# Weight rounding rescheduled over two blocks: earlier tiles and three more of them in block 0, one VectorE step per slot in block 1

## The chip, the cores and the metric

The kernel runs on one core of a Trainium2 chip. The metric is device time in microseconds (us), the median of several runs. A core has TensorE (PE; its weight loads are listed as PEld), VectorE (DVE), ScalarE (ACT), GpSimd (POOL) and SyncE (SP), which here issues most transfers. Each has a queue of its own that it works through in order.

## The reference

An attention without softmax, a normalisation, and two matrix products with a leaky relu between them:

```python
kv = np.einsum('bhsd,bhse->bhde', k, v)          # 8 batches, 8 heads, 576 tokens, 64 wide
out = np.einsum('bhsd,bhde->bhse', q, kv)
rms = np.sqrt(np.mean(out * out, axis=-1, keepdims=True) + 1e-06)
x = (out / rms * g_norm)                          # rearranged to 4608 tokens x 512
h = x @ w_in                                      # 512 x 2048
g = np.maximum(0.01 * h, h)
return g @ w_out                                  # 2048 x 512
```

All is float32, but the two weight matrices arrive as float64. The kernel turns them into float32 itself, from the two 32-bit halves of each number; it calls that rounding.

## The kernel before

**Blocks and chunks.** The 4608 tokens are worked in nine blocks of 512 (`NT`). The 2048 hidden columns are four chunks (`NC`) of 2 x 256. A unit is one block and one chunk: its first product (h), the leaky relu, and its second product (o). Both products are done by a Strassen scheme with seven products in place of eight, so each needs sums and differences of its inputs, made on GpSimd and VectorE.

**Order of the work.** Block 0's chunks 0 to 2 come first, as plain products, in `first_block` (L1120): twelve steps n, each with a group of eight matmuls into `h_ps`, and a group of eight into four accumulators `o_acc` for the step before. Then the loop at L1232 takes block 1 with all four chunks, block 0 with its last chunk, and blocks 2 to 8. A unit of the loop has seven slots, one per Strassen product of h; the o products of earlier units are put between them, after a lag of two slots (`go_o`, L1224). The slot number is `at = 7 * now + t`; the seven products come in the order 1, 2, 6, 5, 7, 3, 4. Products 1, 6, 7 and 4 share one PSUM bank, and 2, 5 and 3 another. Product 5 begins its bank afresh, so it waits until product 2 has been read from it.

**Rounding.** There are 32 jobs (`w_jobs`), each for 128 x 512 weights: 0 to 23 for chunks 0 to 2, 24 to 27 for chunk 3's `w_out`, 28 to 31 for its `w_in`. A job (`round_f64`, L245) is loaded raw by SP (`load_w`), then takes six instructions: two on ScalarE (L263 `add`, L261 `cut`), VectorE L265, ScalarE L270, VectorE L280 and L283. `round_w` (L315) issues the first three and then finishes the job before; `finish_w` issues the rest. In block 0 a table `plan` says what is issued in each half step (n, 0) before and (n, 1) after the o group's place: a number is a job, "f" is `finish_w`, "t" and "a" are steps of two attention generators, "x" is the set of differences of block 1's tokens (`sides_x`). In block 1, `W_SLOTS` lists the slots at which a job is begun; in other slots `finish_w` is called. The group for step n of block 0 needs job 2n-1 for h, and o_acc of step m needs job 2m+2.

**Attention for batch 1** is a generator of steps: transposes of q (`turn`, L500), k-v products, `copy_kv` (L368), two `outputs` (L403), and `divide` (L423): two transposes with reductions, a root (L433), a reciprocal with two spreads, then twice a transpose and a product (L447, L449).

**GpSimd.** Its work for block 1 begins with L1191, a one-element copy that waits for the last of the differences of `sides_x`. Then come the Strassen sums of the weights (`sides_w1`, L699; `sides_w2`, L735), a second level of them (`combine`, L778), which is written to DRAM for the later blocks, and the sums of each unit's g (`sums_of`, L915). In block 1, GpSimd's instructions keep program order. `combine` puts its sums into places listed in `stage_homes`; its third part is done by VectorE at the slots of `DIRECT`.

**Order on the engines.** `pin` keeps an instruction in program order on its engine. The rest (many copies and additions to o) are put between by a planner at compile time, by its own cost estimates. The roundings and the additions to g (L937 to L945) are pinned.

**Homes of the raw weights.** `raws` are seven places of 4 KB per partition (three in `stage`, four in `pairs`), used in turn for jobs 0 to 23; later jobs use two halves of `early`, a token tile that is free by then, and places of `stage`.

Of the kernel before, what the change touches and what calls it, by code (L numbers as in the profile page):

```python
# [24 lines left out]
def kernel(  # L25
# [36 lines left out]
    nc = tc.nc  # L62
# [12 lines left out]
    NC = DF // 2 // (U * P)  # L75
# [37 lines left out]
    def view(t, lo, *shape):  # L113
        n = 1
        for d in shape:
            n *= d
        t = t[:, lo:lo + n]
        names = "abcd"[:len(shape)]
        return t.rearrange(f"p ({' '.join(names)}) -> p {' '.join(names)}",
                           **dict(zip(names, shape))) if len(shape) > 1 else t  # L120
# [97 lines left out]
    def spare(n, name, dtype=F32):  # L218
# [4 lines left out]
    raws = [view(stage, i * NW, NW) for i in range(3)] + [pair(i, NW) for i in range(4)]  # L223
    raw_homes = itertools.chain(
        itertools.islice(itertools.cycle(raws), 4 * K * U),
        itertools.cycle([early[:, :NW], early[:, NW:], raws[0], raws[1], raws[2]]))

    def load(t, src, eng):

# [71 lines left out]
    def load_w(j, *eng):  # L301
        eng = eng or (nc.sync,)
        dst, src = w_jobs[j]
        if w_in.dtype == I64:
            w_raws[j] = load_f64(src.bitcast(U32), eng)
        else:
            load(dst, src, eng)
# [115 lines left out]
    def divide(lo, hi, sums):  # L423

        x, n = x_of(lo, hi), hi - lo
        rms = work.tile([P, 2, n // E], F32, tag="rms", name="rms", bufs=2)
        for l in range(2):
            t = t2k(n, "turned")
            in_turn(nc.vector.transpose(t, sums[l]))
            in_turn(nc.vector.tensor_reduce(rms[:, l, :], t.rearrange("p (a i) -> p a i", i=E),  # L430
                                            axis=AX.X, op=ALU.add))
            if l:
                act = nc.scalar.activation(rms, rms, func=AF.Sqrt, scale=1.0 / D, bias=eps_sb)  # L433
                if first_done or in_first:
                    pin(act)
            yield
        in_turn(nc.vector.reciprocal(rms, rms))
        spread = []
        for l in range(2):
            t = t2k(n, "spread")  # L440
            first_turn(nc.scalar.copy(t.rearrange("p (a i) -> p a i", i=E),
                                      rms[:, l, :].unsqueeze(2).to_broadcast([P, n // E, E])))
            spread.append(t)
        yield
        for l in range(2):
            inv = t2k(n, "inv")
            in_turn(nc.vector.transpose(inv, spread[l]))  # L447
            to = x[:, 2 * l:2 * l + 2, :]
            in_turn(nc.vector.tensor_mul(to, to, inv.unsqueeze(1).to_broadcast([P, 2, n])))  # L449
            yield  # L450
# [243 lines left out]
    def add(eng, out_, a, b_, minus=False, pinned=False):  # L694
        ins = eng.tensor_tensor(out_, a, b_, op=ALU.subtract if minus else ALU.add)  # L695
        if pinned or steady or (in_block_1 and eng is nc.gpsimd):
            pin(ins)
# [37 lines left out]
    def sides_w2(n):  # L735
# [7 lines left out]
        def sums(i):  # L743
# [15 lines left out]
            else:  # L759
# [12 lines left out]
    NG = 7 * P  # L772
    SLOT = {1: 0, 2: 1, 4: 2, 5: 3, 6: 4, 7: 5, 3: 6}
    w1_dram = [dram.tile([P, 7, 7, P], F32, name=f"w1_{c}") for c in range(NC)]
    stage_homes = iter([view(w1_all, (6 + i) * NW, NW) for i in (0, 1, 0, 1)]
                       + [view(stage, i * NW, NW) for i in (1, 2, 0, 1, 2, 0, 1, 2, 0, 1, 2, 0)])

    def combine(c, part):  # L778


        direct = w1_sb[0][c].rearrange("p u (t r) m -> p u r t m", t=2)
        last = w1_sb[1][c][:, :, 2:, :].unsqueeze(3)
        parts = [((5, 6), pair(0, U, 2, 2, P))], [((7, 3), pair(1, U, 2, 2, P))], \
            [((1, 2), direct), ((4,), last)]

        eng = nc.vector if part == 2 else nc.gpsimd
        for js, y in parts[part]:
            t = view(next(stage_homes), 0, 4, len(js), P)
            s1, s2, s3, s4 = (t[:, i, :, :] for i in range(4))
            y11, y12, y21, y22 = (y[:, u, r, :, :] for u in range(2) for r in range(2))  # L790

            add(eng, s1, y21, y22, pinned=part == 2)
            add(eng, s2, s1, y11, True, pinned=part == 2)
            add(eng, s3, y11, y21, True, pinned=part == 2)
            add(eng, s4, y12, s2, True, pinned=part == 2)
            to = w1_dram[c][:, :, AT[js[0]]:AT[js[0]] + len(js), :]
            if js[0] == 1:
                for r in range(2):
                    put_off(to[:, r, :, :], y[:, 0, r, :, :])
            else:  # L800
                put_off(to[:, :2, :, :], y[:, 0, :, :, :])
            put_off(to[:, 2, :, :], y22)
            put_off(to[:, 3:, :, :], t)
# [316 lines left out]
    def first_block(between):  # L1120
# [27 lines left out]
        for t in range(4):  # L1148
# [8 lines left out]
    tail, a_steps = tail_of(0, NT, S, True), attention(1, False)  # L1157
    t, a, f, x = "tafx"
    plan = {(1, 0): (5, f, t), (1, 1): (t, 6, f, t), (2, 0): (t, 7, f, t), (2, 1): (8, f, t, t),
            (3, 0): (9, f, a), (3, 1): (10, f), (4, 0): (11, f, a), (4, 1): (12, f),  # L1160
            (5, 0): (13, f, a), (5, 1): (14, f), (6, 0): (15, f), (7, 0): (16, f, a, a),
            (7, 1): (17, f, a, a), (8, 0): (18, f, a), (8, 1): (19, a, f, a),
            (9, 0): (20, a, f), (9, 1): (21, a, f, a), (10, 0): (22, f), (10, 1): (23, f, x)}
    loaded, x_sides = 12, None

    def between(n, half):
        nonlocal loaded, x_sides
        for what in plan.get((n, half), ()):
            if what == f:
                finish_w()  # L1170
            elif what == x:
                x_sides, _, sums, _ = sides_x(1)
                go(sums)
            elif what in (t, a):
                go(tail if what == t else a_steps, 1)
            else:
                round_w(what)
                to = what + 7 if what < 19 else what + 5
                while loaded <= min(to, 28):
                    load_w(loaded)  # L1180
                    loaded += 1
                    if loaded in (13, 16):
                        load_pair(1, {13: 2, 16: 3}[loaded], homes=homes_1[{13: 2, 16: 3}[loaded]])
# [2 lines left out]
    first_block(between)  # L1186
    in_first = False
    first_done = True
    rounded = 24
    in_block_1 = True  # L1190
    pin(nc.gpsimd.tensor_copy(pair(0, NW)[:1, :1], x_sides[4][:1, 0, :1]))  # L1191
    h_sides, more = sides_w1(0)
# [4 lines left out]
        sides_w2(0)[1](part)  # L1197
    in_loop = True

    W_SLOTS = (1, 3, 5, 7, 10, 11, 13, 14)  # L1200
    LATE_ONE = {15: 2, 16: 1}
    A_SLOTS = {18: 1, 19: 1, 20: 1, 23: 1, 24: 1, 25: 1, 26: 1, 27: 1, 28: 1, 29: 1, 34: 2}
    DIRECT = {15: 0, 20: 1, 23: 2, 26: 3}
    READS = {20: 2, 24: 4, 28: RING}
    PARTS = {33: ("11", "12"), 35: ("22",), 37: ("21",)}

# [25 lines left out]
    for i, chunks in rounds:  # L1232
# [7 lines left out]
        for c in chunks:  # L1240
# [4 lines left out]
                product_h_two(i, c, now, quarters, g_sides, second_of(now - 2))  # L1245
            for t in range(7):
                slot = 7 * c + t
                go(h_steps, 1)
                if not one:

# [39 lines left out]
                    read(READS[at])  # L1290
                if one:
                    if at in DIRECT:
                        combine(DIRECT[at], 2)
                    if t == 3 and nxt[0] < 2 and nxt[1] != c:
                        h_sides, more_h = sides_w1(nxt[1])
                        combine(nxt[1], 0)
                    if t == 5 and nxt[0] < 2 and nxt[1] != c:
                        more_h()
                        combine(nxt[1], 1)
                    if at in W_SLOTS:  # L1300
                        round_w(rounded)
                        rounded += 1
                        if loaded < len(w_jobs):
                            load_w(loaded)
                            loaded += 1
                    else:
                        finish_w()
                    if at in (15, 16):
                        load_pair(2, at - 15)
                    go(late, LATE_ONE.get(at, 0))  # L1310
                    go(a_steps, A_SLOTS.get(at, 0))
                    load_some()
                    if at == 7 * NC - 4:
                        x_sides, _, sums, _ = sides_x(0)
                        go(sums)
                    elif at == 7 * N1 - 4:
                        x_sides, new_quarters, sums, inner = sides_x(2)
                        go(sums)
                    elif at == 7 * N1 - 3:
                        inner(0)  # L1320
                    elif at == 7 * N1 - 2:
                        inner(1)
# [44 lines left out]
```

## Time and profile before

| what | value |
|---|---|
| median of 3 runs | 932.97 us (932.75 to 933.2) |
| profiled execution: time, span | 932.04 us, 930.3 us |
| mean granted TensorE clock | 0.998 |
| PE, PEld busy | 909.7 us (98%), 784.5 us (84%) |
| VectorE, ScalarE, GpSimd busy | 628.6 us (68%), 347.3 us (37%), 375.7 us (40%) |
| TensorE works on block 0's steps | from 24.6 to 120.9 us |
| block 1's first h group begins | 120.88 us |

The span runs from the first to the last instruction of the profiled execution; its own time is a little longer. An engine's busy share is a mean over stages with different limits, so the stages are read one by one. A line such as "PE a L1 <- DVE b L2" says that a TensorE instruction writing `a` waited and that VectorE's instruction at L2, writing `b`, came last. In a list by time the columns are start, duration, engine, line, operation, output, input, shape, number, and in brackets the idle time before it. L126 is the helper that records every matmul and L695 the one that records every addition, so these are told apart by the tiles they write.

### The profile page before, as it was taken

What the parts mean: (1) busy time and instruction counts of PE and PEld (TensorE: products, weight loads), DVE (VectorE), ACT (ScalarE), POOL (GpSimd) and SP (SyncE); (2) the same over time, 40 slices, a digit from 0 to 9 for tenths busy, and PEclk for the clock granted to TensorE, in tenths of its full rate; (3) what the DMA queues carried; (4) which work ended last, traced back from release to release, by engine and by line L of the source; (5) the groups of instructions that cost most, each with busy time, mean ns of one, the idle gap of its engine ahead of it and who ended that gap; (6) DMA issues with size and microseconds to landing.
All of it is one profiled execution on the core that took longest, in us unless ns stands there. A gap on an engine that the chain in (4) does not pass through costs nothing.

```text
span 930.3 us, 18159 instructions
## 1 busy us (share of the span) xinstructions
PE 909.7 (98%) x7024; PEld 784.5 (84%) x7024; DVE 628.6 (68%) x1151; ACT 347.3 (37%) x679; POOL 375.7 (40%) x443
## 2 busy tenths in 40 slices
PE   8998889899999999999999999999999999999998
PEld 4543368688898999999999999999999999999997
DVE  5673745978575877577856786688658755765565
ACT  5764545313234422433334324333343333223330
POOL 2000199864623275226322632255225622552222
PEclk9999999999999999999999999999999999999999
DMA  9996264599689678877887778757765676567632
GB/s 253 243 266 183 68 216 165 180 336 311 206 277 312 212 227 251 249 236 223 252 259 230 215 222 263 234 176 219 238 187 172 188 225 199 185 187 219 200 116 91
DMA packets 92405, 202.16 MB, mean 217 GB/s; under 512 B 10016, under 2 KB 44448, under 8 KB 92320
## 3 DMA queue, kind: packets, MB, share of 16 engines
q1 hardware_dynamic: 81344, 189.14, 68.3%
q10 hardware_dynamic: 10528, 10.69, 3.4%
q8 instruction: 56, 0.92, 0.4%
q0 software_dynamic: 448, 1.18, 0.3%
q14 instruction: 29, 0.24, 0.1%
HBM read 173.44 MB, written 27.53 MB: 216 GB/s over the span
## 4 chain that ended last, share of the span: by engine, by line
PE 81%; DMA 8%; DVE 6%; ACT 2%; issue 1%; SPq 1%; POOL 0%; DVEq 0%; ACTq 0%; POOLq 0%
PE o_c L126 18%; PE o_a L126 18%; PE h_ha L126 11%; PE h_hb L126 10%; PE h_hc L126 8%; PE h_hd L126 8%; PE o_ps L126 3%; DMA v_in<-in_v_dram 2%; DMA q_in<-in_q_dram 1%; DMA pairs<-in_moe_w_in_dram 1%; DMA stage<-in_moe_w_in_dram 1%; PE h_a L126 1%; DMA pairs<-in_v_dram 1%; PE h_c L126 1%; DVE g L695 1%
## 5 line engine op out<-in xcount | busy, mean ns | idle before, releaser
L695 POOL TENSOR_TENSOR gs<-g 128x512 f32<-128x512 f32 x66 | 85.3, 1292 | 255.7 <-ACT g L908 255.7
L908 ACT ACTIVATE g<-g 128x512 f32<-128x512 f32 x127 | 80.1, 631 | 142.0 <-DVE g L695 142.0
L1027 ACT COPY w_all<-h_ha 128x512 f32<-128x512 f32 x84 | 49.0, 583 | 169.2 <-PE h_ha L126 163.6
L126 PE MATMUL o_c<-pairs,gs 128*128 128x256 f32 x392 | 93.3, 381 | 1.8 <-DVE o L695 1.8
L126 PE MATMUL o_a<-pairs,gs 128*128 128x256 f32 x392 | 93.0, 380 | 0.0
L695 DVE TENSOR_TENSOR o<-h_hb,o 128x128 f32<-128x128 f32 x104 | 29.9, 287 | 83.4 <-ACT pairs L1027 83.3
L126 PEld LDWEIGHTS o_c<-pairs,gs 128*128 128x128 f32 x392 | 71.2, 190 | 11.6 <-issue 2.2
L695 DVE TENSOR_TENSOR o<-o_a,o 128x512 f32<-128x512 f32 (+1 forms) x93 | 62.5, 672 | 23.7 <-PE o_a L126 23.3
L126 PEld LDWEIGHTS o_a<-pairs,gs 128*128 128x128 f32 x392 | 71.3, 190 | 8.1
L695 DVE TENSOR_TENSOR o<-o_c,o 128x512 f32<-128x512 f32 x80 | 54.7, 684 | 25.4 <-PE o_c L126 25.2
L126 PE MATMUL h_ha<-stage,w_all 128*128 128x128 f32 x448 | 59.6, 276 | 0.0
L126 PEld LDWEIGHTS h_ha<-stage,w_all 128*128 128x128 f32 x448 | 56.6, 192 | 3.0 <-issue 0.7
L695 DVE TENSOR_TENSOR g<-g,pairs 128x512 f32<-128x512 f32 x84 | 55.7, 689 | 1.9
L695 POOL TENSOR_TENSOR pairs<-g 128x128 f32<-128x128 f32 x52 | 23.8, 458 | 75.9 <-PE h_hb L126 47.4
L695 DVE TENSOR_TENSOR w_all<-h_hc,w_all 128x512 f32<-128x512 f32 x56 | 38.4, 685 | 15.9 <-PE h_hc L126 15.8
L695 DVE TENSOR_TENSOR o<-h_hd,o 128x128 f32<-128x128 f32 x78 | 22.2, 284 | 38.0 <-ACT pairs L1027 37.9
L126 PE MATMUL h_hb<-stage,w_all 128*128 128x128 f32 x336 | 46.7, 275 | 0.0
L126 PE MATMUL o_acc<-w,g 128*128 128x512 f32 x96 | 43.8, 599 | 2.9 <-DVE w L283 2.9
L695 POOL TENSOR_TENSOR gs<-g,gs 128x512 f32<-128x512 f32 x33 | 45.8, 1386 | 0.0
L695 POOL TENSOR_TENSOR gs<-gs,g 128x512 f32<-128x512 f32 x33 | 44.6, 1351 | 2.6
L1027 ACT COPY pairs<-h_hb 128x384 f32<-128x384 f32 x84 | 40.1, 477 | 13.6 <-PE h_hb L126 13.2
L126 PE MATMUL h_ps<-xT,w_all 128*128 128x512 f32 (+1 forms) x104 | 44.0, 569 | 0.1
(242 smaller groups left out, 2237.2 us busy)
## 6 DMA issues: line engine op xcount, KB each, us to landing
w_all<-w SPq DMA_DIRECT2D x196, 448.0 KB, 4.2
pairs<-w SPq DMA_DIRECT2D x56, 512.0 KB, 4.4
out_dram<-o ACTq DMA_DIRECT2D x35, 256.0 KB, 4.5
v_in<-in_v_dram SPq DMA_DIRECT2D x27, 288.0 KB, 4.9
k_in<-in_k_dram SPq DMA_DIRECT2D x26, 288.0 KB, 4.3
q_in<-in_q_dram SPq DMA_DIRECT2D x52, 144.0 KB, 5.7
q_in<-in_q_dram SPq DMA_DIRECT2D x52, 140.0 KB, 5.7
stage<-in_moe_w_out_dram SPq DMA_DIRECT2D x8, 512.0 KB, 6.7
```

The source lines that it names most:

```text
L126: pin(nc.tensor.matmul(*args, **kw))
L695: ins = eng.tensor_tensor(out_, a, b_, op=ALU.subtract if minus else ALU.add)
L908: nc.scalar.activation(t, t if src is None else src, func=AF.Prelu, alpha=SLOPE)
L1027: nc.scalar.copy(q[:, at], bank)
```

## The change

The table for block 0 is rewritten. Job 16 goes to the half step (6, 1), which was empty, and each later job one half step earlier; from (7, 0) on, the attention steps stand ahead of the job in their half step, not behind it. The root of `divide` becomes a step of its own while block 0 runs. Jobs 24, 25 and 26 are done in steps 11 and 12. The raw weights of jobs from 24 on use three homes in turn, where it was five; `combine`'s second and third places become two of `stage`, where they were in `w_all`. In block 1 the five jobs left are begun in slots 0, 3, 6, 9 and 12: L263, L261 and L265 in the first slot, L270 ahead of the h product of the second and L280 behind it, L283 in the third. VectorE's part of `combine` is split in two over two slots, the differences of `sides_x` likewise, and the rest of batch 1's attention moves from slots 15 and 16 to 17 and 19.

```diff
-        itertools.cycle([early[:, :NW], early[:, NW:], raws[0], raws[1], raws[2]]))
+        itertools.cycle([early[:, :NW], early[:, NW:], raws[0]]))
...
             if l:
+                if in_first:
+                    yield
                 act = nc.scalar.activation(rms, rms, func=AF.Sqrt, scale=1.0 / D, bias=eps_sb)
...
-    stage_homes = iter([view(w1_all, (6 + i) * NW, NW) for i in (0, 1, 0, 1)]
-                       + [view(stage, i * NW, NW) for i in (1, 2, 0, 1, 2, 0, 1, 2, 0, 1, 2, 0)])
+    stage_homes = iter([view(w1_all, (6 + i) * NW, NW) for i in (0, 1)]
+                       + [view(stage, i * NW, NW) for i in (1, 2, 1, 2, 0, 1, 2, 0, 1, 2, 0, 1, 2, 0)])
...
-            [((1, 2), direct), ((4,), last)]
-
-        eng = nc.vector if part == 2 else nc.gpsimd
+            [((1, 2), direct)], [((4,), last)]
+
+        eng = nc.vector if part > 1 else nc.gpsimd
...
-            (3, 0): (9, f, a), (3, 1): (10, f), (4, 0): (11, f, a), (4, 1): (12, f),
-            (5, 0): (13, f, a), (5, 1): (14, f), (6, 0): (15, f), (7, 0): (16, f, a, a),
-            (7, 1): (17, f, a, a), (8, 0): (18, f, a), (8, 1): (19, a, f, a),
-            (9, 0): (20, a, f), (9, 1): (21, a, f, a), (10, 0): (22, f), (10, 1): (23, f, x)}
+            (3, 0): (9, f, t, a), (3, 1): (10, f), (4, 0): (11, f, a), (4, 1): (12, f),
+            (5, 0): (13, f, a), (5, 1): (14, f), (6, 0): (15, f), (6, 1): (16, f),
+            (7, 0): (a, a, 17, f), (7, 1): (a, 18, f), (8, 0): (a, 19, f), (8, 1): (a, 20, f),
+            (9, 0): (a, a, 21, f), (9, 1): (22, a, f), (10, 0): (a, 23, a, f), (10, 1): (a, x),
+            (11, 0): (24, f), (11, 1): (25, f), (12, 1): (26, f)}
...
-                to = what + 7 if what < 19 else what + 5
-                while loaded <= min(to, 28):
+                to = what + 7 if what < 17 else max(24, what + 3)
+                while loaded <= min(to, 31):
...
-    rounded = 24
+    rounded, rest = 27, collections.deque()
...
-    W_SLOTS = (1, 3, 5, 7, 10, 11, 13, 14)
-    LATE_ONE = {15: 2, 16: 1}
+    LATE_ONE = {17: 2, 19: 1}
...
-    DIRECT = {15: 0, 20: 1, 23: 2, 26: 3}
+    DIRECT = {15: 0, 16: 1, 20: 2, 21: 3, 22: 4, 23: 5, 26: 6, 27: 7}
...
+                if rest:
+                    go(steps, rest[0][0])
                 go(h_steps, 1)
...
-                        combine(DIRECT[at], 2)
+                        combine(DIRECT[at] // 2, 2 + DIRECT[at] % 2)
...
-                    if at in W_SLOTS:
-                        round_w(rounded)
+                    if not rest and rounded < len(w_jobs):
+                        steps = rounding(rounded)
+                        rest.extend(((0, 3), (2, 1), (0, 1)))
                         rounded += 1
-                        if loaded < len(w_jobs):
-                            load_w(loaded)
-                            loaded += 1
-                    else:
-                        finish_w()
+                    if rest:
+                        go(steps, rest.popleft()[1])
+                    if loaded < min(rounded + 3, len(w_jobs)):
+                        load_w(loaded)
+                        loaded += 1
...
-                        go(sums)
                     elif at == 7 * N1 - 4:
                         x_sides, new_quarters, sums, inner = sides_x(2)
-                        go(sums)
-                    elif at == 7 * N1 - 3:
+                    if at in (7 * NC - 4, 7 * NC - 3, 7 * N1 - 4, 7 * N1 - 3):
+                        go(sums, 2)
+                    if at == 7 * N1 - 3:
                         inner(0)
```

More of the change, by code (lines that the diff above doesn't have):

```diff
@@ L790, in combine @@
             y11, y12, y21, y22 = (y[:, u, r, :, :] for u in range(2) for r in range(2))
[L792 to L795, printed above, removed]
+            add(eng, s1, y21, y22, pinned=part > 1)
+            add(eng, s2, s1, y11, True, pinned=part > 1)
+            add(eng, s3, y11, y21, True, pinned=part > 1)
+            add(eng, s4, y12, s2, True, pinned=part > 1)
             to = w1_dram[c][:, :, AT[js[0]]:AT[js[0]] + len(js), :]
```

## The prediction

> **What bounds the kernel now.** I read the page first, then the busy time by stretch, then TensorE's own waits, then VectorE's and GpSimd's instructions in order of time in block 0 and block 1.
>
> Busy time by stretch (length of the stretch; busy time and number of instructions of PE, PEld, DVE, ACT, POOL; granted clock; DMA share; GB/s):
>
> ```profile
> 60.00:121.00 61.00, 54.77 (x219) 22.98 (x218) 34.94 (x56) 29.00 (x52) 7.87 (x7) 0.97 0.53 142
> 121.00:149.20 28.20, 24.85 (x114) 20.82 (x113) 16.55 (x18) 15.24 (x27) 27.57 (x27) 1.00 0.79 250
> 149.20:181.00 31.80, 27.58 (x155) 23.30 (x154) 22.73 (x35) 13.79 (x29) 27.60 (x24) 1.00 0.40 129
> 181.00:215.00 34.00, 33.51 (x285) 28.74 (x285) 28.16 (x46) 6.11 (x10) 21.32 (x20) 1.00 1.04 333
> 215.00:930.00 715.00, 712.15 (x5776) 658.87 (x5774) 488.10 (x921) 246.12 (x491) 286.13 (x355) 1.00 0.72 218
> ```
>
> After 215 us TensorE is busy 712 of 715 us, and the diff touches nothing there. All that can be won lies between 60 and 215 us, where PE is idle 6.2 + 3.4 + 4.2 + 0.5 = 14.3 us. From 121 to 149 us GpSimd (POOL) is busy 27.6 of 28.2 us: it is nearly a second bound. TensorE's waits from 60 to 215 us (us in total, times, longest):
>
> ```profile
> PE o_ps L126 <- DVE kv L370: 3.3, 1, 3.3
> PE o_acc L126 <- DVE w L283: 2.9, 3, 1.4
> PE h_c L126 <- DVE g L695: 2.4, 1, 2.4
> PE h_a L126 <- DVE g L695: 2.2, 1, 2.2
> PE o_c L126 <- DVE o L695: 2.0, 2, 1.8
> PE h_d L126 <- DVE g L695: 0.6, 1, 0.6
> PE h_b L126 <- ACT g L933: 0.6, 1, 0.6
> ```
>
> All but one end with VectorE: its queue runs in program order, and what TensorE wants stands behind roundings. The first is copy_kv (82.02 us) behind roundings 16 and 17 and a 1.25 us transpose. Third and fifth (171.53 and 178.81 us) come when roundings 29 to 31 and the first chunk's combine crowd the queue. Who shares with whom is seen in GpSimd's and VectorE's queues at the start of block 1 (start, us, instruction):
>
> ```profile
> 113.73 1.27 POOL L695 TENSOR_TENSOR pairs<-w_all 128x512 f32<-128x512 f32 x1
> 115.08 1.60 POOL L695 TENSOR_TENSOR pairs<-pairs,w_all 128x512 f32<-128x512 f32 x1
> 116.64 1.71 POOL L695 TENSOR_TENSOR pairs<-w_all 128x512 f32<-128x512 f32 x1
> 118.31 1.27 POOL L695 TENSOR_TENSOR pairs<-w_all,pairs 128x512 f32<-128x512 f32 x1
> ```
> ```profile
> 114.30 1.25 DVE L280 SCALAR_TENSOR_TENSOR w<-cut,w 128x512 uint32<-128x512 uint32 x1 [0.70 <-ACT w L270]
> 115.59 1.64 DVE L283 CUSTOM_DVE_ANT_0 w<-w,add 128x1024 uint16<-128x1024 uint16 x1
> ```
>
> Alone, L280 and L283 take 0.69 us (103.00 and 103.73 us). Beside GpSimd they take 1.25 and 1.64, and GpSimd's 1.27 becomes 1.60 and 1.71.
>
> **What the Trainium skill says.** SBUF — State Buffer, "Who interferes with whom": VectorE and GpSimd share a port pair under "an exclusive lock"; a VectorE operation with two SBUF inputs blocks or is blocked by a reading GpSimd operation, and so is a tensor_scalar in a 2-port mode. The lines above agree. An addition with one input in PSUM is free of it: the g additions stay at 0.68 us. TensorE: Matmul & The Clock Gate, "What's actually happening": after an idle window of about 3.4 us TensorE runs at half clock until a busy one has passed. Here, after the 3.31 us wait, the stretch 82 to 85 us shows a clock of 0.52. The eight matmuls of h_ps at 84.23 took 4.33 us (3.60 otherwise), the first o_ps group 1.94 (0.98). Same page, "Architectural detail": ScalarE and VectorE are strictly first in, first out; the waits above agree.
>
> **The change part by part.**
>
> *Block 0: tiles sooner, attention steps ahead of the rounding.* Job 16 moves into the empty half step (6,1), all later ones half a step sooner; turn 3, its k-v products and copy_kv now stand ahead of roundings 17 and 18. Job 16's raw weights are issued at 63.91 us and take 6.7 us, so are there at 70.6. I walk the queues in program order with the trace's spacings (add and cut 0.57 each, L265 0.34, L270 0.54, L280 0.72 with L283 behind it, L283 0.61). L283 of 16 ends at 74.3, turn 3 at 75.4, L283 of 17 at 78.3, copy_kv at 78.7; TensorE gets there at 78.7 to 82. So the 3.3 us wait and its slow clock (0.96 + 0.73 us) go. From 75.36 us TensorE has ten groups at 3.44 and two o_ps at 0.9: it would end block 0 at 75.36 + 34.4 + 1.8 = 111.5, not 120.88. Roundings 18 to 23 end at 81, 89, 93, 98, 101 and 107.4; the groups that need them (o_acc 7, h 10, o_acc 9, h 11, o_acc 10, o_acc 11) start at 83, 94, 98, 101, 105, 108. The 2.9 us of o_acc waits go too: **9.4 us less up to the end of block 0**.
>
> *Root a step of its own.* One more yield and one more "t" and "a"; the same instructions. L433 (0.32 us) moves behind job 22's add and cut on ScalarE; nothing on the path waits: zero, at worst 1.1 us on ScalarE, covered by its idle time (2.5 us before h 8's relu).
>
> *Three more tiles in block 0 (24 to 26).* Nine ScalarE and nine VectorE instructions and the same DMAs sooner. They stand ahead of the first g addition of block 1, on VectorE, in pinned order. Loads come through three homes in place of five: the load of 27 waits for ScalarE's read of 24, that of 30 for 27's; they stand on SP's queue ahead of write-outs with 4 us of slack. 27's load can go at 106.3 us and takes 5.9, and is wanted at about 117: I take zero; a late one would cost its lateness, on a path with 2 us of slack.
>
> *What this does to GpSimd.* Its block 1 work is released by L1191, after the last of sides_x(1). Before, that ended at 112.67. Now: rounding 22 ends at 100.8, reciprocal, spreads and job 23's add and cut bring L265 of 23 to 103.3, transpose and product to 105.4, one x difference 0.6, L280 and L283 to 107.4, transpose and product 1.75, three differences of 0.6: 111.1. So GpSimd starts only 1.6 us sooner while TensorE comes 9.4 us sooner. From 113.73 to 147.45 us GpSimd never pauses: 30 operations up to gs's second sum, which TensorE's third o group of unit 0 reads at 149.19. Those 33.7 us hold about 4.3 us above the unhindered spacing (1.35, 1.23, 0.81, 0.68 us), with 14 rounding instructions of VectorE beside them: 0.31 us each. After: 24, 25, 26 less one L265 (8) and slots 0 to 11 (12), 20 or 21, say 21: seven more, 2.2 us, so 35.9 us. gs is ready at 112.2 + 35.9 = 148.1 us.
>
> *VectorE's backlog.* Beside GpSimd about one rounding instruction fits per GpSimd operation. The eight left and slot 0's take nine operations, to 124; then the g addition of slot 1, for which the h group of slot 3 waits (its bank): TensorE, there at 117, idles some 8 us and restarts at about 124.8 with half clock (1.7 to 3.4 us lost). Six h groups, then h, o, h, o, h (1.73 each, with o from slot 9) bring it to the third o group at 145.5 to 147. GpSimd's 148.1 is later. So of 9.4 us won in block 0, 8.4 are given back: **1.0 us gained by the third o group (148.2 against 149.19)**.
>
> *One VectorE step per slot.* Jobs 27 to 31 use slots 0 to 14; the waits at 171.53 and 178.81 and the gap at 164.82 (2.40 + 1.82 + 0.33 = 4.55 us) came from roundings up to 178 us. They go, because VectorE has no rounding after slot 14. The h addition of slot 15 stands ahead of combine's, now 4 + 4 additions in two slots of 3.45 us (0.41 or 0.28 us alone, up to 1.49 beside GpSimd). I take **4.1 gained**, leaving 0.4 for combine.
>
> *Combine's homes and split, x differences two per slot.* Same instructions, thinner: zero from 181 us on, where only 0.5 us is idle. Home w_all 6 is rewritten by job 28 in slot 4, after its write-out (landing about 128); a late one blocks ScalarE by 1 to 2 us, inside the 2 us of slack.
>
> Sum: 1.0 + 4.1 = 5.1 us. The profiled execution took 932.04 us (span 930.3), so 926.9. The median of the runs is 932.97, 0.93 more: **927.9 us**.
>
> **Rivals.** *The lock is dearer (slower).* If the planner leaves the x differences behind rounding 24 (GpSimd from 113.7 as before) and each of 21 instructions costs GpSimd its full 0.6 us, gs comes at 113.7 + 29.4 + 12.6 = 155.7. The third o group starts 6.5 us later, 4.1 come back: 2.4 slower, 935.4. It decides from 0.5 us each. For it: 0.65 us stolen by the pair shown above, GpSimd's fullness; against: the mean of 0.31.
>
> *The late waits stay.* Combine and the tail of attention fill VectorE in slots 15 to 19 beside GpSimd, and 171.5 and 178.8 wait for them instead: only 1.0 gained, 932. For it: combine's 8 additions took 5.2 us; against: they now stand behind the h addition.
>
> *GpSimd is not hindered further.* gs at 145.9, TensorE itself bounds at 146.5: 2.7 + 4.5 = 7.2 gained, 925.7; with no cold clock either and lighter sharing, 923. For it: VectorE can fit into gaps between GpSimd's operations (L265's price was as low as 0.07).
>
> **How the numbers follow.** Likeliest 0.40 (925.9 to 930.5), GpSimd free 0.20, late waits stay 0.17, lock dearer 0.23. A measurement of this kernel tells 0.2% (1.9 us) from no change. Faster 0.61, same 0.16, slower 0.23. The range reaches from the free case's 923.5 to the dear lock's 935.5.
>
> **What would show it.** Right: no wait of o_ps for kv, clock 1.00 at 82 us, block 0's last o_acc ending near 111.5; L1191 near 111.2; then h_c waiting several us for DVE g with a half clock after it, and an o_a wait for POOL gs near 148; no PE wait above 1 us from 150 to 215. Wrong: GpSimd's release later than 113, gs's second sum after 151, waits for DVE o or g after 160 us, or a new wait of an o_acc for L283.

## The result and the profile after

The changed kernel takes 931.95 us (median of 20 runs, 928.51 to 934.45), the kernel before 931.89 us on the same chip (20 runs): a ratio of 0.9997 (95%: 0.9987 to 1.0008), no difference. The forecast was 927.9 us. The profiled execution took 931.65 us (span 929.9; before 932.04, span 930.3).

In the changed kernel's lines the numbers are two higher, from `divide` on: the helper of the additions is L697, the copy of h_a L935.

Two fixed points make the two traces comparable: the start of block 1's first h group (slot 0), and the start of the third o group of unit 0, the first that needs GpSimd's sums gs.

| stretch | before | after | difference |
|---|---|---|---|
| span's start to o_acc of step 6 | 75.36 us | 74.42 us | -0.94 (there already at block 0's first group, 22.94 against 23.87 us) |
| from there to slot 0 | 45.52 | 36.66 | -8.86 |
| slot 0 to the third o group | 28.31 | 38.81 | +10.50 |
| third o group to the end | 781.11 | 780.01 | -1.10 |

So block 0's gain came nearly in full, and was lost within the next 39 us; and the last stretch, which should have won 4.1 us, won 1.1. The first row is scatter of the start: over all profiled executions of this document block 0's first group begins between 22.70 and 23.87 us. Differences below 1 us between starts in two traces are therefore taken for effects only where both started alike, as the changed kernel, x1_unsplit, x7_homes, x9_warm_half and x12_split_homes did (22.93 to 23.03).

Busy time by stretch of the changed kernel, columns as in the prediction's view of it:

```profile
60.00:112.00 52.00, 52.00 (x220) 22.98 (x220) 33.02 (x55) 30.76 (x56) 1.46 (x2) 1.00 0.60 151
112.00:149.20 37.20, 27.93 (x106) 22.88 (x105) 22.38 (x25) 17.36 (x31) 36.44 (x32) 0.86 0.66 212
149.20:181.00 31.80, 31.80 (x229) 27.43 (x232) 24.31 (x33) 11.35 (x24) 28.61 (x27) 1.00 0.69 213
181.00:215.00 34.00, 31.01 (x229) 26.56 (x220) 23.92 (x42) 4.84 (x8) 18.43 (x17) 0.95 0.90 288
```

TensorE never pauses from 60 to 112 us and from 149 to 181 us. Between them it is idle 9.3 us at a mean clock of 0.86, and after 181 us it is idle 3.0 us at 0.95. Its waits from 60 to 215 us (us in total, times, longest):

```profile
PE h_d L126 <- DVE g L697: 5.1, 2, 3.0
PE h_c L126 <- DVE g L697: 3.9, 1, 3.9
PE h_a L126 <- POOL w_all L697: 3.3, 1, 3.3
```

The groups that waited, by time, with the third o group (149.89):

```profile
117.95 1.97 PE L126 MATMUL h_a<-xt,pairs 128*128 128x256 f32 x8 [3.26 <-POOL w_all L697]
123.77 3.78 PE L126 MATMUL h_c<-xt,pairs 128*128 128x256 f32 x8 [3.85 <-DVE g L697]
...
142.92 3.40 PE L126 MATMUL h_d<-xt,pairs 128*128 128x256 f32 x8 [2.16 <-DVE g L697]
...
149.89 1.89 PE L126 MATMUL o_a<-pairs,gs 128*128 128x256 f32 x8
...
198.41 3.43 PE L126 MATMUL h_d<-xt,pairs 128*128 128x256 f32 x8 [2.99 <-DVE g L697]
```

A group of eight takes 1.89 to 1.99 us at full clock. Three of these take 3.40 to 3.78: TensorE runs at half clock there (the last section shows when). The third o group itself does not wait: GpSimd had gs ready at 145.94 us, 4 us sooner.

```profile
144.67 1.27 POOL L697 TENSOR_TENSOR gs<-gs,g 128x512 f32<-128x512 f32 x1
```

Thus GpSimd, which I took for the bound, was not it. Nor did it end the wait of h_a: ScalarE's copy that empties the bank came last.

```profile
116.17 0.65 ACT L263 ACTIVATE add<-stage 128x512 uint32<-128x512 uint32 x1
116.73 0.66 ACT L261 ACTIVATE cut<-stage 128x512 f32<-128x512 f32 x1
117.29 0.57 ACT L935 COPY g<-h_a 128x512 f32<-128x512 f32 x1
```

What stood ahead of the late h_d group, in VectorE's order (start, duration):

```profile
196.07 0.87 DVE L697 TENSOR_TENSOR stage<-w_all 128x128 f32<-128x128 f32 x1
196.97 0.29 DVE L697 TENSOR_TENSOR stage<-stage,w_all 128x128 f32<-128x128 f32 x1
197.18 0.29 DVE L697 TENSOR_TENSOR stage<-w_all 128x128 f32<-128x128 f32 x1
197.38 0.28 DVE L697 TENSOR_TENSOR stage<-w_all,stage 128x128 f32<-128x128 f32 x1
197.58 0.68 DVE L697 TENSOR_TENSOR g<-h_d,g 128x512 f32<-128x512 f32 x1
```

The first four, 1.5 us in all, are the second half of combine, as the change splits it; the fifth empties the bank that the h_d group begins afresh. The product that it reads had ended at 190.24 us, so it ran 7 us after it could have. In the kernel before, combine's additions around this slot began right behind that g addition (194.37 and 194.98 us).

And ahead of the h_d group at 142.92 us, ScalarE's order:

```profile
134.38 0.67 ACT L263 ACTIVATE add<-stage 128x512 uint32<-128x512 uint32 x1
134.95 0.67 ACT L261 ACTIVATE cut<-stage 128x512 f32<-128x512 f32 x1
135.62 0.59 ACT L935 COPY g<-h_b 128x512 f32<-128x512 f32 x1
136.10 0.63 ACT L270 ACTIVATE w_all<-cut 128x512 int32<-128x512 f32 x1
```

and VectorE's behind it:

```profile
136.77 1.13 DVE L280 SCALAR_TENSOR_TENSOR w_all<-cut,w_all 128x512 uint32<-128x512 uint32 x1 [5.51 <-ACT w_all L270]
137.82 0.68 DVE L697 TENSOR_TENSOR g<-h_c,g 128x512 f32<-128x512 f32 x1
```

Job 28's L270 needs VectorE's cut, which was there at 130.7 us, but it stands behind two steps of job 29, which the program issues two slots later. `pin` does not forbid that: it ties an instruction only to the one issued just before it on its engine, and where unpinned copies come between, later ones may be laid ahead of it. VectorE stands still 5.5 us at job 28's L280, with pinned g additions behind it. L270 writes into w_all 6, the place that combine's first sums leave by a transfer issued at 126.32 us; such transfers landed in 3.6 us, so it was over by 130 us.

### The profile page after: what moved, and what is told of

The parts are those of the page before. It is cut to its first block, busy times and chain, and to the rows that moved or that the text cites. A ratio compares the mean times of both kernels' runs of the same rounds, so it can differ in the third digit from the quotient of the medians.

```text
span 929.9 us, 18153 instructions
## 1 busy us (share of the span) xinstructions
PE 911.9 (98%) x7024; PEld 788.7 (85%) x7024; DVE 632.4 (68%) x1151; ACT 347.7 (37%) x679; POOL 375.8 (40%) x443
## 4 chain that ended last, share of the span: by engine, by line
PE 85%; DMA 8%; DVE 4%; ACT 2%; issue 1%; POOL 0%; SPq 0%; ACTq 0%; DVEq 0%; POOLq 0%
PE o_c L126 19%; PE o_a L126 18%; PE h_ha L126 11%; PE h_hb L126 10%; PE h_hc L126 8%; PE h_hd L126 8%; PE o_ps L126 3%; PE h_a L126 2%; PE h_c L126 2%; DMA stage<-in_moe_w_out_dram 2%; DMA pairs<-in_moe_w_in_dram 1%; PE h_d L126 1%; PE h_b L126 1%; DMA pairs<-in_v_dram 1%; DMA pairs<-in_moe_w_out_dram 1%
## 5 line engine op out<-in xcount | busy, mean ns | idle before, releaser
L697 POOL TENSOR_TENSOR gs<-g 128x512 f32<-128x512 f32 x66 | 85.2, 1291 | 254.9 <-ACT g L910 254.9
L697 DVE TENSOR_TENSOR o<-h_hb,o 128x128 f32<-128x128 f32 x104 | 29.8, 287 | 83.6 <-ACT pairs L1029 83.5
L697 DVE TENSOR_TENSOR o<-o_a,o 128x512 f32<-128x512 f32 (+1 forms) x93 | 62.5, 672 | 21.0 <-PE o_a L126 20.6
L697 DVE TENSOR_TENSOR o<-o_c,o 128x512 f32<-128x512 f32 x80 | 54.7, 683 | 27.5 <-PE o_c L126 26.2
L697 DVE TENSOR_TENSOR g<-g,pairs 128x512 f32<-128x512 f32 x84 | 55.7, 689 | 1.9
L697 POOL TENSOR_TENSOR pairs<-g 128x128 f32<-128x128 f32 x52 | 23.8, 458 | 75.8 <-PE h_hb L126 47.4
L697 DVE TENSOR_TENSOR w_all<-h_hc,w_all 128x512 f32<-128x512 f32 x56 | 38.3, 685 | 15.9 <-PE h_hc L126 15.8
L697 DVE TENSOR_TENSOR o<-h_hd,o 128x128 f32<-128x128 f32 x78 | 22.1, 283 | 38.1 <-ACT pairs L1029 38.0
L697 POOL TENSOR_TENSOR gs<-gs,g 128x512 f32<-128x512 f32 x33 | 44.3, 1341 | 2.6
L697 POOL TENSOR_TENSOR gs<-g,gs 128x512 f32<-128x512 f32 x33 | 45.2, 1369 | 0.0
L126 PE MATMUL h_hd<-xT,w_all 128*128 128x128 f32 x224 | 43.3, 275 | 0.0
```

Of the source, the lines that this page charges most:

```text
L126: pin(nc.tensor.matmul(*args, **kw))
```

## The experiments

A letter in an expectation names the theory that it then spells out. "DIRECT" is the table of slots at which VectorE does its part of combine. Medians are of the timed runs, ratios against runs of the kernel before on the same chip.

**x1_unsplit: the changed kernel with combine's two halves in one slot again.**

```diff
-    DIRECT = {15: 0, 16: 1, 20: 2, 21: 3, 22: 4, 23: 5, 26: 6, 27: 7}
+    DIRECT = {15: 0, 20: 1, 23: 2, 26: 3}
...
-                        combine(DIRECT[at] // 2, 2 + DIRECT[at] % 2)
+                        combine(DIRECT[at], 2)
+                        combine(DIRECT[at], 3)
```

> The changed kernel with VectorE's part of combine in one slot per chunk again (slots 15, 20, 23, 26); nothing else differs. Theory L (late wait): in the changed kernel the second half of chunk 1's combine stands in slot 21, directly ahead of the g addition of slot 22, which is kept behind it; that addition then runs at 197.6 us, and h_d waits 3.0 us at 198.4 and restarts at half clock (1.5 us more). Unsplit, the wait goes: span about 929.9 - 4.4 = 925.5 us, no TensorE wait over 1 us from 150 to 215 us. Rival: the wait comes from the attention tail moved to slots 17 and 19 or from TensorE's earlier arrival; then it stays, and the span is 930 us.

Measured: 927.19 us, ratio 0.9942 (0.9920 to 0.9964), span 925.3. TensorE in the last stretch but one:

```profile
181.00:215.00 34.00, 34.00 (x268) 28.82 (x260) 28.33 (x46) 7.95 (x17) 23.05 (x20) 1.00 1.03 326
```

The wait at 198 us and its half clock are gone, the third o group is where it was (149.92 us), and 4.6 us of span are won. What changed is an order, not an amount of work:

```profile
190.46 0.69 DVE L697 TENSOR_TENSOR g<-h_d,g 128x512 f32<-128x512 f32 x1 [0.37 <-PE h_d L126]
...
196.18 0.87 DVE L697 TENSOR_TENSOR stage<-w_all 128x128 f32<-128x128 f32 x1
```

The second half of combine runs when it did (196.07 us in the changed kernel), but the g addition is no longer tied behind it and runs 7 us sooner.

**x2_split_alone: the kernel before with that split alone.**

```diff
-    DIRECT = {15: 0, 20: 1, 23: 2, 26: 3}
+    DIRECT = {15: 0, 16: 1, 20: 2, 21: 3, 22: 4, 23: 5, 26: 6, 27: 7}
...
```

> The kernel before, with combine's VectorE part split over two slots (15, 16, 20 to 23, 26, 27) and nothing else. Theory L: a wait of h_d for DVE g of 2 to 3 us appears near 199 us with up to 1.7 us of half clock; span 933 to 935 us. Rival (the split is harmless by itself): 930 us, as before, no such wait.

Measured: 938.78 us, ratio 1.0063 (1.0040 to 1.0087), span 934.6 (before 930.3).

```profile
204.58 1.75 PE L126 MATMUL h_d<-xt,pairs 128*128 128x256 f32 x7 [3.49 <-DVE g L695]
```

The same group waits for the same addition. The split is harmful without the rest of the change.

**x3_block0_alone: the kernel before with block 0's new order and the root step only**; jobs 24 to 26 stay in block 1. The table is the change's without its last line:

```diff
...
+            (9, 0): (a, a, 21, f), (9, 1): (22, a, f), (10, 0): (a, 23, a, f), (10, 1): (a, x)}
...
             if l:
+                if in_first:
+                    yield
```

> The kernel before with the new order of block 0 (jobs 16 to 23 half a step sooner, attention steps first, root apart), but with jobs 24 to 26 left in block 1 and block 1 as before. Theory B (backlog): TensorE enters block 1 at 111.1 us and meets no rounding backlog, so the group of slot 3 does not wait; GpSimd, released near 110.5, then bounds: gs's second sum 33.7 us later, at 144.4, and the third o group at about 144.7 (before 149.2, changed 149.9). The waits of before at 171 and 179 us stay: span about 926 us. Rival G (GpSimd and ScalarE alone eat the gain whatever VectorE does): third o group at 149 or later, span 930 us.

Measured: 928.09 us, ratio 0.9954 (0.9938 to 0.9970), span 927.8. Its waits:

```profile
PE o_a L126 <- POOL gs L697: 4.0, 1, 4.0
PE h_b L126 <- POOL pairs L697: 3.2, 1, 3.2
PE h_c L126 <- DVE g L697: 2.2, 1, 2.2
PE h_a L126 <- DVE g L697: 1.1, 1, 1.1
```

Here GpSimd is the bound: the third o group starts at 144.80 us, after waiting 4.0 us for gs. Two stretches of half clock come with it (144.12 to 150.95 us) and after it (171.43 to 174.84), and the rest of the span is 783.0 us, 1.9 longer than before's. So the tiles that are done sooner are worth 0.46% by themselves, where the whole change is worth nothing.

**x4_two_tiles: the changed kernel with job 26 left in block 1** (slots 0 and 1).

```diff
-            (11, 0): (24, f), (11, 1): (25, f), (12, 1): (26, f)}
+            (11, 0): (24, f), (11, 1): (25, f)}
...
-    rounded, rest = 27, collections.deque()
+    rounded, rest = 26, collections.deque()
...
-                        rest.extend(((0, 3), (2, 1), (0, 1)))
+                        rest.extend(((0, 3), (2, 2)) if rounded == 26 else ((0, 3), (2, 1), (0, 1)))
```

> The changed kernel with two tiles (24, 25) in block 0 in place of three; job 26 takes slots 0 and 1, jobs 27 to 31 three slots each, to slot 16. Theory B: one job less stands ahead of slot 1's g addition, so h_c of slot 3 starts about 3 us sooner than 123.8 and one window of half clock (1.7 us) less is paid; the third o group at 146 to 148 us (changed 149.9); the late wait near 198 stays: span 927 to 929 us. Rival G: no gain, 930 us.

Measured: 933.13 us, ratio 1.0011 (0.9998 to 1.0024), span 929.7. The h_c group of slot 3 starts at 120.68 us, 3.1 sooner, and the third o group at 146.23, 3.7 sooner. Nothing is left of it: the late h_d wait, behind the split combine, grew from 2.99 to 5.28 us, with half clock after it. Time won early is lost again where a later wait is bound to VectorE's order.

**x5_two_unsplit: the edits of x4_two_tiles and x1_unsplit together.**

> Two tiles in block 0 (as in x4) and combine unsplit (as in x1). Theory L with B: x4's third o group at 146.2 us stays, and its late wait (5.3 us, with two windows of half clock, 3.4 us) goes: span 929.7 - 8.7 = 921 us, 923 at most. Rival: the time lost with the three tiles is paid elsewhere whatever the backlog (GpSimd or ScalarE), and it comes out like x1: 925.3 us.

Measured: 927.81 us (20 runs, 924.91 to 932.86), ratio 0.9963 (0.9951 to 0.9974); a miss. The late h_d wait is gone, but another came:

```profile
205.24 2.04 PE L126 MATMUL kv_ps<-v_in,k_in 64*64 64x64 f32 x65 [3.22 <-DMA v_in<-in_v_dram]
```

Batch 2's k-v products wait for their load: job 26's place in block 1 moves the later roundings on by two slots, and their scratch tiles sit in the buffers of k_in and v_in. The last rounding ends at 174.2 us (161.2 in x7_homes below), the second pair's load is issued at 174.22 (168.37), and the load waited for at 200.10 (192.88). No run takes this chain apart. The profiled execution was the slowest of the 20.

**x6_warm: x1_unsplit with 18 dummy matmuls ahead of the groups that wait**, so that TensorE's clock stays up.

```diff
+    DUMMIES = {2: ("hb", 6), 3: ("hd", 8), 10: ("hc", 4)}
...
+                if 7 * now + t in DUMMIES:
+                    tag, count = DUMMIES[7 * now + t]
+                    idle = ps_m.tile([P, NT], F32, tag=tag, name="idle_ps")
+                    for _ in range(count):
+                        matmul(idle, lhsT=ident, rhs=w2_sb[0][0][:, 0, :], start=True, stop=True)
```

> x1 (changed kernel, combine unsplit) with 18 matmuls added whose results nobody reads: 6 ahead of slot 2's group, 8 ahead of slot 3's, 4 ahead of slot 10's, into banks that are free, about 0.43 us each. They fill TensorE's waits at 118, 124 and 143 us (3.3, 3.9 and 2.1 us) and add nothing to what VectorE and ScalarE do. Theory H (half clock): with the waits filled, no window of half clock comes there, and the matmuls after them run at 1.9 us per group in place of 3.8, 3.1 and 3.3: 3.1 + 1.9 us back unless another engine is then in the way; the third o group at 146 to 148 us (x1: 149.9), span 922 to 924 us. Rival: VectorE and GpSimd set the pace there, so the half clock cost nothing: span 925.3 us as x1.

Measured: 930.6 us, ratio 0.9993 (0.9984 to 1.0002), span 929.2, clock 1.000; a miss by size. A dummy of 128x512 float32 took 0.87 us (two records of 0.43), so the 18 took 15.7 us, against 9.2 us of waits in x1_unsplit, and the third o group came at 153.56. It showed only that the half clock can be removed.

**x7_homes: x1_unsplit with combine's first two homes in stage** too, none in w_all.

```diff
-    stage_homes = iter([view(w1_all, (6 + i) * NW, NW) for i in (0, 1)]
-                       + [view(stage, i * NW, NW) for i in (1, 2, 1, 2, 0, 1, 2, 0, 1, 2, 0, 1, 2, 0)])
+    stage_homes = iter([view(stage, i * NW, NW)
+                        for i in (1, 2, 1, 2, 1, 2, 0, 1, 2, 0, 1, 2, 0, 1, 2, 0)])
```

> x1 with the places of combine's first two results moved from w_all 6 and 7 to two of stage, so that no write-out from w_all 6 is under way when job 28 writes its weights there. Theory W: in the changed kernel L270 of job 28 stands behind job 29's first two steps and runs at 136.1 us, because the planner sees it wait for that write-out; VectorE's L280, the g addition at 137.8 and the one at 142.2 come late behind it, and h_d waits 2.1 us at 143 with a window of half clock. With other places, L270 of job 28 comes near 130 us, that wait and its half clock (1.9 us) go: third o group at 146 to 147 us, span 921.5 to 923 us. Rival: the wait at 143 comes from the backlog of 24 to 26 alone; it stays, 925.3 us.

Measured: 924.55 us (923.87 to 925.35), ratio 0.9928 (0.9913 to 0.9942), span 922.1. It beats the kernel before by 6.9 us (931.4 on the same chip). Job 28 on ScalarE:

```profile
129.57 0.64 ACT L270 ACTIVATE w_all<-cut 128x512 int32<-128x512 f32 x1 [1.53 <-DVE cut L265]
```

It stands 6.5 us sooner, ahead of job 29's steps; VectorE's g addition for h_c follows at 131.15 us (137.82), the one for h_d at 136.88 (142.19), and the h_d wait with its half clock is gone. Now the third o group waits, for GpSimd:

```profile
146.64 1.99 PE L126 MATMUL o_a<-pairs,gs 128*128 128x256 f32 x8 [1.82 <-POOL gs L697]
```

**x8_two_homes: x5_two_unsplit with these homes.**

> x5 with the places of x7. If W also holds with two tiles: L270 and L280 of jobs 28 and 29 come sooner; but there GpSimd's gs already bounds the third o group (146.2 us, wait for POOL gs 1.6 us), so little is left: the same as x5 within 1 us. If W's wait was the bound there too: 1 to 2 us less.

Measured: 928.53 us, ratio 0.9965 (0.9951 to 0.9980), as x5_two_unsplit. The third o group is at 146.12 us, but the wait for v_in remains (1.73 us). The third tile in block 0 is thus not what costs: with it the same kernel takes 924.55.

**x9_warm_half: x6_warm with half of its dummies**, `{2: ("hd", 3), 3: ("hd", 4), 10: ("hc", 2)}`; the homes are those of the change.

> x1_unsplit with 9 dummy f32 products of 128x512 on TensorE, half of x6's number, because each took 0.87 us there (two records of 0.43): 3 ahead of slot 2's group, 4 ahead of slot 3's, 2 ahead of slot 10's, into the bank that the group itself starts anew; their results are read by nobody. Theory H (part of the missing time is TensorE at half clock behind its waits): the waits are filled by the dummies, no half-clock window is left, the third o group starts at 146 to 148 us (x1_unsplit: 149.9) and the span is 922 to 924 us. Rival: VectorE and GpSimd set the pace there and TensorE's clock is only a symptom: 925.3 us, as x1_unsplit.

Measured: 924.11 us, ratio 0.9909 (0.9876 to 0.9941), span 922.1, clock 1.000.

```profile
119.89 3.60 PE L126 MATMUL idle_ps<-w,ident 128*128 128x512 f32 x8
123.89 1.99 PE L126 MATMUL h_c<-xt,pairs 128*128 128x256 f32 x8 [0.40 <-DVE g L697]
...
146.71 1.99 PE L126 MATMUL o_a<-pairs,gs 128*128 128x256 f32 x8 [1.50 <-POOL gs L697]
```

Adding work that nobody reads won 3.2 us of span over x1_unsplit: the slow clock behind the waits is a loss of its own. A new order of the rest is not the reason: job 28's L270 still stands behind two steps of job 29 (133.31 us), and VectorE still stands still for 5.0 us at its L280. And the third o group starts at 146.71 us with the wait for gs again, as in x7_homes.

**x10_release: x7_homes with GpSimd released by the first x difference.**

```diff
-    pin(nc.gpsimd.tensor_copy(pair(0, NW)[:1, :1], x_sides[4][:1, 0, :1]))
+    pin(nc.gpsimd.tensor_copy(pair(0, NW)[:1, :1], x_sides[5][:1, 0, :1]))
```

> x7_homes with GpSimd's release copy waiting for the first x difference of block 0 instead of the last: GpSimd's run of slots starts some 4.7 us sooner (near 106 instead of 110.7 us). Theory G (GpSimd's start bounds what is left: the wait for gs is 1.8 us in x7_homes): the third o group starts up to 1.8 us sooner (some 144.8 us) and the span is near 920.5 us. Rival (the two engines share access to SBUF): VectorE's last differences and products of block 0 run beside GpSimd's and get longer, TensorE enters block 1 later, and the span is 922 us or more.

Measured: 927.23 us, ratio 0.9945 (0.9925 to 0.9964), span 926.3: slower than x7_homes, the rival. GpSimd started at 107.07 us in place of 110.49, though the whole execution started 0.8 us later. VectorE's last product and differences of block 0:

```profile
108.03 1.75 DVE L451 TENSOR_TENSOR xT<-xT,inv 128x896 f32<-128x896 f32 x1
109.82 1.64 DVE L697 TENSOR_TENSOR xt<-xT,xt 128x512 f32<-128x512 f32 x1
111.38 1.75 DVE L697 TENSOR_TENSOR xT<-xT 128x512 f32<-128x512 f32 x1
113.05 1.75 DVE L697 TENSOR_TENSOR xt<-xT,xt 128x512 f32<-128x512 f32 x1
```

They take 1.09 and 0.69 us in x7_homes; beside GpSimd's sums (1.27 to 1.99 us each) they wait for one each. That is what the Trainium skill's SBUF — State Buffer, "Who interferes with whom", says of two engines with one lock, here in both directions. VectorE is 4.5 us late with the next rounding, ScalarE behind it, and the h_a group of slot 2 starts at 121.84 us (118.05; 0.8 us of each delay is the later start). Half clock from 120.92 to 134.57 us goes with it.

**x11_homes_warm: x7_homes with seven dummies**, `{2: ("hd", 3), 3: ("hd", 4)}`.

> x7_homes with 7 of the dummy products (3 ahead of slot 2's group, 4 ahead of slot 3's); their results are read by nobody. x7_homes and x9_warm_half both wait for gs ahead of the third o group (1.8 and 1.5 us) and both have a span of 922.1 us. Theory G (GpSimd's sums set the pace once the rest is mended): TensorE waits longer for gs, the third o group starts at 146.5 to 146.9 us as in both, and the span is 922 us within 0.7. Rival (the two repairs add up): the 3.4 us lost to half clock in x7_homes come back, third o group near 144, span 919 to 920 us.

Measured: 927.32 us, ratio 0.9956 (0.9941 to 0.9970), span 925.4: neither.

```profile
147.65 2.91 PE L126 MATMUL o_a<-pairs,gs 128*128 128x256 f32 x8 [4.06 <-POOL gs L697]
150.36 2.70 PE L126 MATMUL h_d<-xT,pairs 128*128 128x256 f32 x8
```

GpSimd is the bound, as theory G has it: TensorE waits 2.2 us longer than in x7_homes for the same sums. The group starts 1.0 us later, since GpSimd started 0.45 later and its sums took 0.6 longer. The miss is that the one wait is now long enough for half clock (1.8 us lost).

**x12_split_homes: the changed kernel with x7_homes' homes alone**, that diff put into the changed kernel.

> The changed kernel with x7_homes' two homes, combine still split over two slots. Theory (the losses by the split and by the homes are separate): third o group at 146.7 us (changed kernel 149.89), the late wait for g in slot 22 of 2 to 3 us and its half clock stay, span 926 to 927.5 us, some 4 to 5 us above x7_homes. Rival (the time won early by the homes makes TensorE wait longer later): the late wait grows by what is won, span 929 us or more.

Measured: 929.16 us, ratio 0.9980 (0.9968 to 0.9992), span 925.7. The third o group starts at 146.58 us, as expected, and the late wait stays:

```profile
195.61 1.97 PE L126 MATMUL h_d<-xt,pairs 128*128 128x256 f32 x8 [3.40 <-DVE g L697]
```

The homes bring the third o group forward by 3.3 us with the split (149.89 to 146.58) and without it (149.92 to 146.64), so the two losses are separate. That size is read from the traces: by the ratios the homes are worth some 1.6 us with the split and 1.3 without, and the intervals overlap. In the profiled execution this wait was followed by no half clock, so its span lies below the range expected; the median span of its nine runs, 927.4 us, does not.

All profiled executions in one table: when the third o group starts, and the rest of the span after it.

| kernel | third o group | rest | what is late in the rest |
|---|---|---|---|
| before | 149.19 us | 781.1 us | waits behind roundings up to 178 us |
| after | 149.89 | 780.0 | h_d behind the split, half clock |
| x1_unsplit | 149.92 | 775.4 | nothing |
| x2_split_alone | 149.58 | 785.0 | waits as before, h_d behind the split |
| x3_block0_alone | 144.80 | 783.0 | half clock, h_c behind roundings |
| x4_two_tiles | 146.23 | 783.5 | h_d behind the split, half clock |
| x5_two_unsplit | 146.97 | 784.1 | v_in, half clock |
| x6_warm | 153.56 | 775.6 | nothing |
| x7_homes | 146.64 | 775.5 | nothing |
| x8_two_homes | 146.12 | 780.9 | v_in, half clock |
| x9_warm_half | 146.71 | 775.4 | nothing |
| x10_release | 150.97 | 775.3 | nothing |
| x11_homes_warm | 147.65 | 777.8 | half clock |
| x12_split_homes | 146.58 | 779.1 | h_d behind the split |

Five kernels without a late loss agree on the rest within 0.3 us. So a time is its third o group's start, plus 775.4, plus the late waits: the changed kernel loses 3.2 us by the first against x7_homes and 4.6 by the last.

## Why the prediction was wrong

**Block 0, "9.4 us less": right.** 8.86 us measured from o_acc of step 6 to slot 0, which starts at 111.08 us (111.5 forecast), with no o_ps or o_acc wait and a clock of 1.00.

**GpSimd: right in size, wrong as the bound.** Its release came at 110.40 us (forecast 111.1), its first sum at 110.69 (112.2), and gs was ready 35.3 us after that (35.9). But TensorE came later still. The third o group, forecast for 148.2 us, came at 149.89.

**"VectorE's backlog": the restart was right, what follows it was short.** TensorE was forecast to idle some 8 us and restart at 124.8. It idled 7.1 us in two waits and restarted at 123.77, behind VectorE's g addition as forecast. The first of them, which the profile puts down to GpSimd, ended with ScalarE's copy of h_a (L935, 117.29 us), which stood behind jobs 25's and 26's steps; I had walked VectorE's queue and not ScalarE's.

**"A late one blocks ScalarE by 1 to 2 us, inside the 2 us of slack": failed.** Nothing blocked at run time; the planner laid job 28's step behind job 29's, at 136.10 in place of 129.57 us. The wait of 2.16 us and the half clock behind it (the three groups from 142.92 us up to the third o group took 6.97 us, 5.18 at full clock) come to 4.0 us, of which 3.2 count against x7_homes, where gs comes at 146.6. Undoing the homes won 3.2 us of span (the profiled executions of x7_homes and x1_unsplit; by the ratios less, as said at x12_split_homes). The order alone did not make this loss: x9_warm_half keeps it, but not the half clock after the restart, which cost 3.0 us (the two groups from 123.77 us took 6.47, 3.45 at full clock), and gets as far. So the loss took both.

**"One VectorE step per slot, 4.1 gained": right, and under-sized.** Without the split the rest of the span is 5.7 us shorter than before (775.4 against 781.1). No run parts this step from the three tiles that left block 1.

**"Combine's homes and split: zero from 181 us on": failed, and decided the result.** I counted the split's instructions and not their places. Four additions came to stand directly ahead of the pinned g addition for which a bank, and so TensorE, was waiting; it ran 7 us later, and that cost 4.6 us of span (x1_unsplit), 0.63% when put into the kernel before (x2_split_alone). I had looked only for idle time that was there already, not at what the moved instructions would stand in front of.

The sum: forecast span 925.2, measured 929.9. The third o group is 1.7 us later than forecast and the rest wins 3.0 us less; together 4.7. With both failed steps undone the span is 922.1, because gs came 1.5 us sooner than forecast (146.6 against 148.1) and the last stretch won 1.6 more. That is close in number to the rival "GpSimd is not hindered further", but not by its mechanism: GpSimd's sums took 35.8 us in x7_homes, as I had forecast (35.9), and only began sooner (110.79 against 112.2). Of the other rivals, "the late waits stay" came nearest in size (932), but by another mechanism: not combine's amount of work, only its order. "The lock is dearer" did not come about.

**What stays open.** Whether GpSimd's 36 us, the bound of x7_homes, can be shortened was not tried; to begin them sooner failed (x10_release). In x7_homes 3.3 us of waiting for ScalarE's copy and 2.5 for VectorE are left, and by x11_homes_warm, where filling them only made the wait for gs longer, they cost nothing while GpSimd is the bound. The planner's reason for job 28's place was not looked into; that the homes decide it is shown.

## What to carry to other kernels

Price a moved or split instruction by what it then stands in front of on its engine, above all ahead of an operation that empties a PSUM bank; four additions of 1.5 us in all cost 4.6 us that way. Where a chain and an engine beside it end within 2 us of each other, as TensorE and GpSimd do here, walk each queue between, ScalarE's too, and hold a buffer's new reader against the planned place of its next writer. A gain is worth only what the next floor leaves: three repairs met GpSimd's at 146.6 us, and the fourth made a longer wait of it.

## What the runs showed of the hardware

**Half clock goes by fixed windows, not by the length of one wait.** The Trainium skill's TensorE: Matmul & The Clock Gate, "What's actually happening", puts the slow-down after about one idle window of 3.4 us and calls the windows free-running. Here stretches of half clock last 3.41 us or a multiple of it, but they followed single waits of 2.16 us (changed kernel, 142.92) and 2.09 us (x1_unsplit), and did not follow 3.40 us (x12_split_homes) or 3.49 us (x2_split_alone). The traces tell why. In the changed kernel half clock begins at 122.87, 143.35 and 197.96 us, 6 and 16 times 3.413 us apart, and in each other trace with several stretches the edges lie on such a grid too. Cut on its own grid, the changed kernel's wait falls into one window, and that of x12_split_homes into two (changed kernel first; columns as above, TensorE's busy time second, its clock third from the end):

```profile
139.93:143.35 3.42, 1.26 (x6) 0.79 (x5) 2.72 (x4) 1.56 (x3) 3.34 (x5) 1.00 0.34 115
143.35:146.76 3.41, 3.41 (x10) 2.70 (x9) 1.18 (x2) 2.19 (x5) 3.33 (x3) 0.50 0.46 154
```
```profile
190.57:193.99 3.42, 1.64 (x8) 1.11 (x6) 1.79 (x4) 0.54 (x1) 3.42 (x4) 1.00 1.03 396
193.99:197.40 3.41, 1.79 (x8) 1.63 (x9) 1.48 (x4) 0.63 (x1) 0.32 (x1) 1.00 1.06 371
197.40:200.82 3.42, 3.42 (x17) 3.02 (x16) 3.17 (x5) 0.58 (x1) 0.00 (x0) 1.00 1.11 367
```

Idle for 2.16 us of a window, TensorE has half clock in the next; idle for 1.78 and 1.62 us of two, it keeps its clock. From 60 to 215 us in all fourteen traces, a window at full clock with more than 1.96 us idle (busy time as the profile has it) was always followed by one at half clock, one with less than 1.73 us never; between the two both happened. So a wait of 2 us or more can cost a window or nothing, by where it falls, which differs from one execution to the next. Each window costs at most 1.7 us, half its length. They are a likely part of the spread: the changed kernel's runs at a mean clock of 0.994 took 928.5 to 931.6 us, those at 0.989 from 933.0 to 934.5.

**Dummy work can pay.** Nine products that nobody reads, 7.8 us of TensorE, shortened a kernel bound by TensorE by 3.2 us (x9_warm_half); eighteen made it 3.9 us longer in span (x6_warm), and seven, beside the new homes, 3.3 us longer than those alone (x11_homes_warm).
